# Reading both parts of a bank's maxima in a row, one transpose per quad, and a new table of the order of work

## The chip, the cores and the metric

The kernel runs on one core of a Trainium2 chip. The metric is the device time of one execution in microseconds; a kernel's time is the median over its runs. A core has a matrix engine (TensorE, PE in the profile), three engines for element-wise work (VectorE, or DVE; ScalarE, or ACT; GpSimd, or POOL), an engine that here only issues transfers (SyncE, or SP), and 16 DMA engines. PEld is the loading of weights into TensorE. Matrix products land in PSUM, which has eight banks of 128 partitions x 512 float32 values.

## What is computed

Two attention blocks, A and B, of the same shape work on the same input x (2048 tokens x 640 features); their outputs are mixed by a gate per token. Each block has 32 heads of 20 features and goes through four segments of 512 tokens. Within a segment there is causal softmax attention; across segments a small memory per head is read and updated.

```python
x = A_x
g = _sigmoid((x * gate_w).sum(-1, keepdims=True))
a = _A_ref(x, A_wq, A_wk, A_wv, A_wo, A_beta)
b = _B_ref(x, B_wq, B_wk, B_wv, B_wo, B_beta)
return g * a + (1 - g) * b

# within _A_ref and _B_ref, for each of the N = 4 segments s:
qs, ks, vs = q[:, :, s], k[:, :, s], v[:, :, s]
logits = jnp.einsum("bhqd,bhkd->bhqk", qs, ks) * scale + mask
p = _softmax(logits, axis=-1)
a_dot = jnp.einsum("bhqk,bhkd->bhqd", p, vs)
pq = phi(qs)
num = jnp.einsum("bhld,bhde->bhle", pq, M)
den = jnp.einsum("bhld,bhd->bhl", pq, z)[..., None] + 1e-6
a_mem = num / den
o = g * a_mem + (1.0 - g) * a_dot          # here g = sigmoid(beta), one per head
pk = phi(ks)
M = M + jnp.einsum("bhld,bhle->bhde", pk, vs)
z = z + jnp.einsum("bhld->bhd", pk)
```

## The kernel before

**Windows, quads, slots.** A window is one segment of one block, so there are eight windows. The 32 heads of a window are worked on in eight quads of four heads, so there are 64 quads, numbered 0 to 63. The kernel goes through 66 slots, and in slot i, TensorE does the "T units" of quad i and the "S units" of quad i + 2 (`LEAD` is 2), with "fill" work in between: the projections to q, k and v, the output projections, transposes and the memory's products.

**S units and T units.** Softmax needs each row's maximum before the exponentials. The S units compute the scores of a quad with queries on the partitions, only to find those maxima. A quad has five S units for each half of the array (rows 0 to 63 and 64 to 127 of TensorE's array work side by side, as two lanes); a unit fills one PSUM bank, with one part (512 columns) or two parts (384 and 128, or 256 and 256 columns). VectorE reads each part with one operation that adds the causal mask and takes the maximum (line 1268), which the profile shows as an operation and a short read of the accumulator. The T units compute the scores again, with keys on the partitions and with the maximum subtracted by two extra rows of the contraction; ScalarE takes the exponential of a bank (line 1357), GpSimd clears what lies above the diagonal (line 1358), and the product with the values follows in the next slot (line 1385).

**The way of the maxima.** When all ten banks of a quad's S units are read, `m_unit` splits the maxima into a high part (ScalarE, line 1292) and a low part (GpSimd, line 1293) in a tile `mt` of 128 partitions x 32. `m_ready` then waits for one of two small buffers `mr` of 32 partitions x 128. `turn_rows` has VectorE transpose `mt` into `mr` by four operations of 32 x 32 (line 1304), and `send_rows` has SP issue two transfers that put the rows into the two extra rows of q's tile (line 1316). From then on the quad's T units may run.

**How the order is made.** All instructions are emitted by a planner that runs while the kernel is built. It keeps a clock of its own. `put(engine, cost, emit, then, prio)` queues work on an engine's list (A, D, G, S for ScalarE, VectorE, GpSimd, SP): a free engine takes the entry with the lowest priority number, is counted busy for `cost`, and `then` runs a little later, by 0.26 us on VectorE. `dma` does the same for SP. `at(time, fn)` runs a function at a time of the planner's clock. Each engine on the chip carries out its instructions in the emitted order. So the costs set the order, and the chip's real durations set the time.

**The table.** For each slot `RULES` has the order of its five S and five T units as ten letters, and seven numbers: over what share of the slot they are spread, a load of VectorE above which late work isn't started, two delays for transposes' second halves, spare rows, how much earlier than its mark the slot begins, and how long late work may wait.

**Two reads of a bank.** In `s_unit`, `look` is called when a bank's products are done. With two parts, the read of the second is only put on VectorE's list after the first has ended:

```python
if len(todo) > 1:
    one(*todo[0], lambda: (one(*todo[1], read), read()))
else:
    one(*todo[0], read)
```

**The betas.** Each block's 32 betas are loaded into all partitions near the kernel's start (line 1768, priority 15), and `head_gates` (lines 645 to 651) makes the gates from them with ScalarE and VectorE.

Of the kernel before, what the change touches and what calls it, by code (L numbers as in the profile page):

```python
# [12 lines left out]
F32 = mybir.dt.float32  # L13
# [3 lines left out]
ALU = mybir.AluOpType  # L17
# [20 lines left out]
def r32(ap):  # L38
    return ap.bitcast(F32)
# [3 lines left out]
def tile_gated_mix_infini_attn(  # L43
# [44 lines left out]


    RULES = {  # L90
# [66 lines left out]
    }  # L157
    rule = {}
    DONE = {"A": 0.27, "D": 0.26, "G": 0.22, "S": 0.0}
# [10 lines left out]
    def at(time, fn):  # L170
        heapq.heappush(events, (time, next(seq), fn))
# [40 lines left out]
    def put(e, dur, emit, then=None, prio=5):  # L212
        heapq.heappush(ready[e], (prio, next(seq), dur, emit, then))
        load[e] += first_of(dur)
        start_next(e)

    def dma(us, emit, then=None, prio=5, lat=0.9, some=False, issue=0.44):

        def issued():
            dma_free[0] = max(clk[0] + 0.9, dma_free[0]) + us  # L220
            if not some:
                dma_free[0] = dma_free[1] = max(dma_free[0], clk[0] + 0.9 + us, dma_free[1] + us)
            lands.append(dma_free[0] + LANDED)
            if then:
                at(dma_free[0] + lat, then)

        put("S", issue, emit, issued, prio)
# [69 lines left out]
    def then_all(n, fn):  # L297
        left = [n]

        def one():  # L300
            left[0] -= 1
            if not left[0]:
                fn()

        return one
# [944 lines left out]
    def s_unit(i, n):  # L1250
        t, u, q, k = quad(i)
        if n == 0:
            mx[i] = sb.tile([P, 2, 2, NB], F32, tag="mx", name=f"mx{i}", bufs=3)
            s_left[i] = then_all(2 * len(S_UNITS), lambda: m_unit(i))
        todo = S_UNITS[n]
        for half in range(2):
            sc = bank.free.pop(0)
            r = slice(64 * half, 64 * half + 60)

            def look(half=half, sc=sc):  # L1260
                def end():
                    bank.give(sc)
                    s_left[i]()

                read = then_all(len(todo), end)
                def one(pair, qb, off, then):
                    w = P * (qb + 1)
                    put("D", w / 960.0 + 0.105, lambda: nc.vector.tensor_tensor_reduce(  # L1268
                        out=sc[:, off:off + w], in0=sc[:, off:off + w], in1=tri[:, L - w:],
                        scale=1.0, scalar=LOWEST, op0=ALU.add, op1=ALU.max,  # L1270
                        accum_out=mx[i][:, half, pair, qb:qb + 1],
                    ), lambda: at(clk[0] + 0.05, then), prio=3)

                if len(todo) > 1:
                    one(*todo[0], lambda: (one(*todo[1], read), read()))
                else:
                    one(*todo[0], read)

            for j, (pair, qb, off) in enumerate(todo):
                w = P * (qb + 1)  # L1280
                lane_ops[half].append((mm(w), lambda pair=pair, qb=qb, off=off, w=w, r=r, sc=sc: nc.tensor.matmul(  # L1281
                    sc[:, off:off + w], lhsT=q[r, pair, P * qb:P * (qb + 1)], rhs=k[r, pair, 0:w], start=True, stop=True,
                ), look if j == len(todo) - 1 else None))
# [12 lines left out]

    def m_ready(i):
        m_done.add(i)
        mr_store.want(1, lambda mr: put("D", 0.4, lambda: turn_rows(i, mr), lambda: send_rows(i, mr), prio=1), prio=0)

    def turn_rows(i, mr):
        mt = mts.pop(i).rearrange("p f c n -> p (f c n)")
        for j in range(NB):
            nc.vector.transpose(r32(mr[:, 32 * j:32 * j + 32]), r32(mt[32 * j:32 * j + 32, :]))

    def send_rows(i, mr):
        t, u, q, k = quad(i)

        def sent():
            mr_done.add(i)  # L1310
            mr_store.give(mr)

        done = then_all(2, sent)
        for half in range(2):
            r = 64 * half + 60
            dma(0.3, lambda half=half, r=r: nc.sync.dma_start(
                out=r32(q[r:r + 2, :, :].rearrange("p a (b n) -> p (a b) n", b=NB)),
                in_=r32(mr[16 * half:16 * half + 16, :]),
            ), done, prio=-2, some=True, issue=0.68)
# [445 lines left out]
    bts = [const.tile([P, H], F32, name=f"beta{b}") for b in range(2)]  # L1765
    betas_there = then_all(2, lambda: put("D", 0.6, head_gates, prio=6))
    for b in range(2):
        dma(0.9, lambda b=b: nc.sync.dma_start(out=bts[b], in_=betas[b].partition_broadcast(P)), betas_there, prio=15)
    gate_weights()
    at(75.0, lambda: mix_weights(0))  # L1770
    at(215.0, lambda: mix_weights(1))
# [80 lines left out]
```

## Time and profile before

| what | value |
|---|---|
| runs | 987.46, 987.58, 989.22 us; median 987.58 |
| the profiled execution | 989.17 us, of which span 987.4 us |
| granted TensorE clock | 0.999 of full speed |
| TensorE busy | 977.6 us, 99% |
| VectorE busy | 798.8 us, 81% |
| ScalarE busy | 646.9 us, 66% |
| GpSimd busy | 604.0 us, 61% |
| reads of maxima, line 1268 | 1024 operations, 474.5 us, and 1024 reads of the accumulator, 145.2 us |
| transposes of maxima, line 1304 | 256 operations, 51.0 us |

The span goes from the first to the last instruction on the chip. A row of a group reads: line, engine, operation, written tile <- read tiles, shape, count, then busy time in us, the mean of one in ns, and the idle time of the engine just before, with what ended it. A row of waits reads: engine, tile and line that waited <- who ended the wait: us in total, times, longest. A row of the timeline reads: start in us, duration, engine, line, operation; its last part in brackets is the idle time before it and what ended that. Matmuls are pipelined, so one matmul's duration is longer than the time between two starts.

### The profile page before, as it was taken

Reading aid. Unit: us, or ns where it says so; the run is one execution under the profiler, and the core shown is the slowest. Engines: PE = TensorE matmul, PEld = TensorE weight load, DVE = VectorE, ACT = ScalarE, POOL = GpSimd, SP = SyncE. Lnnn points to the kernel's source line nnn. Section 1 sums busy time; section 2 is a strip of 40 time slices with the busy share of each in tenths; the row PEclk is TensorE's granted clock in tenths of the full one; section 3 lists DMA queues with packets and bytes.
Section 4 is the critical chain, followed back from the end, with each engine's and each line's share of the span. In section 5 each row is a group of like instructions: output and inputs, shape, how many; then the busy total and the mean of one; then the engine's idle time right before and its main releaser. Section 6 shows DMA issues by size and latency. Waiting matters only on the chain.

```text
span 987.4 us, 31435 instructions
## 1 busy us (share of the span) xinstructions
PE 977.6 (99%) x11559; PEld 825.5 (84%) x11559; DVE 798.8 (81%) x2825; ACT 646.9 (66%) x1297; POOL 604.0 (61%) x1042
## 2 busy tenths in 40 slices
PE   9999999999999999999999999999999999999998
PEld 7987888788888888897888988887888887879885
DVE  4697888886798888886889878779778898889964
ACT  5366767766667676766776675765667575686582
POOL 4456646955558664776656575566756576566471
PEclk9999999999999999999999999999999999999999
DMA  7998889998897886976769686698577988778531
GB/s 254 303 291 249 280 246 296 258 287 253 258 299 230 281 240 195 313 234 204 225 207 321 191 260 202 212 304 287 166 216 236 276 274 236 219 227 248 147 98 54
DMA packets 146452, 236.47 MB, mean 239 GB/s; under 512 B 12949, under 2 KB 45882, under 8 KB 145978
## 3 DMA queue, kind: packets, MB, share of 16 engines
q1 hardware_dynamic: 146298, 234.46, 77.2%
q8 instruction: 91, 1.49, 0.6%
q14 instruction: 63, 0.52, 0.2%
HBM read 145.26 MB, written 94.65 MB: 243 GB/s over the span
## 4 chain that ended last, share of the span: by engine, by line
PE 93%; DMA 2%; DVE 2%; POOL 1%; ACT 1%; issue 1%; SPq 0%; POOLq 0%; ACTq 0%
PE bank L818 56%; PE bank L1385 14%; PE bank L1365 8%; PE bank L1281 8%; PE bank L929 3%; PE bank L971 3%; PE bank L1029 1%; DMA kst<-kd 1%; PE bank L868 1%; DMA row<-rowg 1%; DMA row<-dots 1%; PE bank L1210 0%; DMA wst<-in_a_wk_dram 0%; POOL p L1358 0%; DVE bank L1268 0%
## 5 line engine op out<-in xcount | busy, mean ns | idle before, releaser
L1268 DVE CUSTOM_DVE_ANT_0 bank<-bank,tri 128x256 f32<-128x256 f32 (+3 forms) x1024 | 474.5, 520 | 90.3 <-PE bank L1281 81.8
L818 PE MATMUL bank<-row,wh 64*128 64x512 f32 x2308 | 487.4, 401 | 0.9 <-ACT p L1357 0.9
L1357 ACT ACTIVATE p<-bank 128x512 f32<-128x512 f32 x546 | 298.8, 604 | 121.9 <-PE bank L1365 102.2
L818 PEld LDWEIGHTS bank<-row,wh 64*128 64x128 f32 x2308 | 315.5, 185 | 15.5 <-ACT p L1357 1.2
L1358 POOL TENSOR_SCALAR_AFFINE_SELECT p<-p 128x256 f32<-128x256 f32 (+1 forms) x546 | 200.0, 376 | 174.5 <-ACT p L1357 161.0
L818 PE MATMUL bank<-row,wl 64*128 64x512 f32 x1154 | 296.9, 398 | 0.0
L555 POOL TENSOR_TENSOR wl<-wst,wh 128x640 fp32r<-128x640 f32 x115 | 181.0, 1579 | 51.7 <-ACT wh L557 41.6
L818 PEld LDWEIGHTS bank<-row,wl 64*128 64x128 f32 x1154 | 173.4, 185 | 5.8 <-issue 0.2
L818 PE MATMUL bank<-wvh,row 64*128 64x320 f32 (+1 forms) x1280 | 177.8, 312 | 0.1
L1365 PE MATMUL bank<-qst,kst 62*128 62x128 f32 (+3 forms) x1024 | 174.9, 319 | 1.3 <-DVE mx L1268 0.7
L1281 PE MATMUL bank<-kst,qst 60*128 60x384 f32 (+3 forms) x1024 | 173.3, 318 | 1.1 <-DMA kst<-kd 1.1
L818 PEld LDWEIGHTS bank<-wvh,row 64*128 64x128 f32 x1280 | 150.4, 185 | 2.0 <-ACT p L1357 0.4
L1268 DVE DVE_READ_ACCUMULATOR2_ANT mx<- 128x1 f32 x1024 | 145.2, 142 | 0.0
L1385 PE MATMUL bank<-p,vst 128*32 128x256 f32 (+3 forms) x1816 | 139.9, 425 | 0.0
L1365 PEld LDWEIGHTS bank<-qst,kst 62*128 62x128 f32 x1024 | 127.1, 186 | 13.8 <-DVE mx L1268 2.9
L1281 PEld LDWEIGHTS bank<-kst,qst 60*128 60x128 f32 x1024 | 126.4, 185 | 11.5 <-DVE mx L1268 2.2
L1385 PEld LDWEIGHTS bank<-p,vst 128*32 128x32 f32 x1816 | 56.6, 110 | 79.7 <-issue 59.5
L818 PE MATMUL bank<-wvl,row 64*128 64x320 f32 (+1 forms) x640 | 105.7, 311 | 0.0
L557 ACT CAST wh<-wst 128x640 fp32r<-128x640 f32 x119 | 87.3, 745 | 20.2 <-PE bank L818 12.8
L818 PEld LDWEIGHTS bank<-wvl,row 64*128 64x128 f32 x640 | 85.2, 186 | 0.7 <-issue 0.2
L1416 ACT COPY row<-bank 128x512 f32<-128x512 f32 x60 | 35.4, 590 | 65.2 <-PE bank L1385 59.5
L530 POOL TENSOR_TENSOR wvl<-wst,wvh 128x640 fp32r<-128x640 f32 (+1 forms) x48 | 60.2, 1260 | 17.6 <-ACT wvh L674 9.2
(119 smaller groups left out, 1131.5 us busy)
## 6 DMA issues: line engine op xcount, KB each, us to landing
qst<-qd SPq DMA_DIRECT2D x128, 240.0 KB
kst<-kd SPq DMA_DIRECT2D x128, 240.0 KB
qd<-row SPq DMA_DIRECT2D x40, 512.0 KB
kd<-row SPq DMA_DIRECT2D x40, 512.0 KB
dots<-row SPq DMA_DIRECT2D x56, 256.0 KB
wst<-wmix SPq DMA_DIRECT2D x35, 320.0 KB
row<-dots SPq DMA_DIRECT2D x42, 256.0 KB
qd<-row SPq DMA_DIRECT2D x40, 256.0 KB
```

The source lines that it names most:

```text
L530: put("G", 0.77 * n, lambda: nc.gpsimd.tensor_tensor(out=wl[:, a:b, :VN], in0=w3, in1=r32(wh[:, a:b, :VN]), op=ALU.subtract), end, prio=4)
L555: put(lo_eng, lo_cost, lambda: lo.tensor_tensor(out=wl, in0=w3, in1=r32(wh), op=ALU.subtract), end, prio=3)
L557: put("A", 0.625, lambda: nc.scalar.copy(wh, w3), low, prio=6)
L818: return nc.tensor.matmul(bank_of, lhsT=w[ROWS[half]], rhs=x_[ROWS[half]], start=start, stop=stop)
L929: return nc.tensor.matmul(pm[:, a - h0:c - h0, :].rearrange("p h e -> p (h e)"), lhsT=r32(pqTs[t, m][ROWS[half], P * n:P * (n + 1)]), rhs= ...
L1268: put("D", w / 960.0 + 0.105, lambda: nc.vector.tensor_tensor_reduce(out=sc[:, off:off + w], in0=sc[:, off:off + w], in1=tri[:, L - w:], s ...
L1281: lane_ops[half].append((mm(w), lambda pair=pair, qb=qb, off=off, w=w, r=r, sc=sc: nc.tensor.matmul(sc[:, off:off + w], lhsT=q[r, pair, P ...
L1357: put("A", 0.483, lambda: nc.scalar.activation(pt, sc, AF.Exp, scale=SCALE), lambda: (bank.give(sc), put("G", 0.15 + 0.105 * len(todo), la ...
L1358: "G", 0.15 + 0.105 * len(todo), lambda: nc.gpsimd.affine_select(out=blocks, in_=blocks, pattern=[[0, len(todo)], [1, P]], base=0, channel ...
L1365: lane_ops[half].append((mm(w), lambda pair=pair, kb=kb, off=off, w=w, r=r, sc=sc: nc.tensor.matmul(sc[:, off:off + w], lhsT=k[r, pair, P ...
L1385: nc.tensor.matmul(po[32 * j:32 * j + 32, P * kb:], lhsT=vst[t % 2][:, kb, h * E1:h * E1 + 32], rhs=pts[i, n, f][0][:, off:off + w], start ...
L1416: either(0.483, lambda: nc.scalar.copy(r32(oT), po), 0.605, lambda: nc.vector.tensor_copy(r32(oT), po), end, 2)
```

## The change

Four things change.

1. The reads of a bank's parts are emitted together, as one entry of VectorE's list, instead of the second after the first.
2. `turn_rows` is one transpose over 128 partitions into a new tile `turned` (128 x 32, three buffers); then a new function `move_rows` copies its four blocks of 32 x 32 side by side into `mr`, two on ScalarE and two on GpSimd. The buffer `mr` is taken after the turn, and the sends follow both engines' copies.
3. The loads of the betas are queued at 16 us of the planner's clock instead of at its start.
4. All 66 rows of the table are others.

```diff
     RULES = {
-        0: "TTTSSTSTSS 1.01 2.38 0.3 8 0 1.6 1",
-        1: "TSTSTSTSTS 1.01 2.38 0.22 8 1.6 1.6 1",
...
+        0: "TSTSTSTSTS 1.01 2.38 0.3 2 0 2.61 1",
+        1: "TTTSSTSTSS 1.01 2.38 0.3 8 0 1.6 1",
...
-                read = then_all(len(todo), end)
-                def one(pair, qb, off, then):
-                    w = P * (qb + 1)
-                    put("D", w / 960.0 + 0.105, lambda: nc.vector.tensor_tensor_reduce(
-                        out=sc[:, off:off + w], in0=sc[:, off:off + w], in1=tri[:, L - w:],
-                        scale=1.0, scalar=LOWEST, op0=ALU.add, op1=ALU.max,
-                        accum_out=mx[i][:, half, pair, qb:qb + 1],
-                    ), lambda: at(clk[0] + 0.05, then), prio=3)
-
-                if len(todo) > 1:
-                    one(*todo[0], lambda: (one(*todo[1], read), read()))
-                else:
-                    one(*todo[0], read)
+                put("D", sum(P * (qb + 1) for _, qb, _ in todo) / 960.0 + 0.125 * len(todo) - 0.02, lambda: [nc.vector.tensor_tensor_reduce(
+                    out=sc[:, off:off + P * (qb + 1)], in0=sc[:, off:off + P * (qb + 1)], in1=tri[:, L - P * (qb + 1):],
+                    scale=1.0, scalar=LOWEST, op0=ALU.add, op1=ALU.max,
+                    accum_out=mx[i][:, half, pair, qb:qb + 1],
+                ) for pair, qb, off in todo], lambda: at(clk[0] + 0.05, end), prio=3)
...
     def m_ready(i):
         m_done.add(i)
-        mr_store.want(1, lambda mr: put("D", 0.4, lambda: turn_rows(i, mr), lambda: send_rows(i, mr), prio=1), prio=0)
-
-    def turn_rows(i, mr):
+        put("D", 0.24, lambda: turn_rows(i), lambda: mr_store.want(1, lambda mr: move_rows(i, mr), prio=0), prio=1)
+
+    turned = {}
+
+    def move_rows(i, mr):
+        done = then_all(2, lambda: send_rows(i, mr))
+        for e, eng, cost, js in (("A", nc.scalar.copy, 0.24, (0, 1)), ("G", nc.gpsimd.tensor_copy, 0.27, (2, 3))):
+            put(e, cost, lambda eng=eng, js=js: [
+                eng(mr[:, 32 * j:32 * j + 32], turned[i][32 * j:32 * j + 32, :]) for j in js], done, prio=1)
+
+    def turn_rows(i):
         mt = mts.pop(i).rearrange("p f c n -> p (f c n)")
-        for j in range(NB):
-            nc.vector.transpose(r32(mr[:, 32 * j:32 * j + 32]), r32(mt[32 * j:32 * j + 32, :]))
+        turned[i] = sb.tile([P, 32], F32, tag="turned", name=f"turned{i}", bufs=3)
+        nc.vector.transpose(turned[i], r32(mt))
...
     for b in range(2):
-        dma(0.9, lambda b=b: nc.sync.dma_start(out=bts[b], in_=betas[b].partition_broadcast(P)), betas_there, prio=15)
+        at(16.0, lambda b=b: dma(0.9, lambda: nc.sync.dma_start(out=bts[b], in_=betas[b].partition_broadcast(P)), betas_there, prio=15))
```

128 rows, old and new, of the table RULES are left out of this document.

## The prediction

> **What bounds the kernel now.** I read the busy shares of the page first, then the groups of TensorE, the order of TensorE in time, and then the waits, engine by engine.
>
> ```profile
> PE 977.6 (99%) x11559; PEld 825.5 (84%) x11559; DVE 798.8 (81%) x2825; ACT 646.9 (66%) x1297; POOL 604.0 (61%) x1042
> ```
>
> TensorE is busy 99% of the span and VectorE is the next engine with 81%. But a busy TensorE need not be a full one. In the next two fences the groups give the counts, and the timeline gives the pitch, the time from one start to the next in a dense run.
>
> ```profile
> L818 PE MATMUL bank<-row,wh 64*128 64x512 f32 x2308 | 487.4, 401 | 0.9 <-ACT p L1357 0.9
> L818 PE MATMUL bank<-row,wl 64*128 64x512 f32 x1154 | 296.9, 398 | 0.0
> L818 PE MATMUL bank<-wvh,row 64*128 64x320 f32 (+1 forms) x1280 | 177.8, 312 | 0.1
> L1365 PE MATMUL bank<-qst,kst 62*128 62x128 f32 (+3 forms) x1024 | 174.9, 319 | 1.3 <-DVE mx L1268 0.7 <-ACT row L987 0.6
> L1281 PE MATMUL bank<-kst,qst 60*128 60x384 f32 (+3 forms) x1024 | 173.3, 318 | 1.1 <-DMA kst<-kd 1.1
> L1385 PE MATMUL bank<-p,vst 128*32 128x256 f32 (+3 forms) x1816 | 139.9, 425 | 0.0
> L818 PE MATMUL bank<-wvl,row 64*128 64x320 f32 (+1 forms) x640 | 105.7, 311 | 0.0
> ```
>
> ```profile
> 20.91 1.35 PE L818 MATMUL bank<-row,wh 64*128 64x512 f32 x10
> 22.07 1.68 PE L818 MATMUL bank<-wvh,row 64*128 64x322 f32 x20
> 23.56 0.64 PE L818 MATMUL bank<-wvl,row 64*128 64x322 f32 x6
> ```
>
> ```profile
> 61.71 2.29 PE bank L1385 x32
> ```
>
> Ten half-array products of 512 columns take 22.07 - 20.91 = 1.16 us, 0.116 each, where the group's mean of one is 401 ns; twenty of 322 columns take 1.49 us, 0.0745 each. At those pitches (2308 + 1154) x 0.116 = 402 us, (1280 + 640) x 0.0745 = 143 us, the 2048 score products, which are 320 columns wide on average (the mean of the widths in the two tables of units), 2048 x 0.0745 = 153 us, and 64 products with the values at 2.29 us (the row of the chain) = 147 us. That is 844 of 987.4 us. The remaining 143 us hold the smaller kinds of matmul, the head, the tail, and the slack: moments in which only one half of the array streams. The Trainium skill, page "Perfetto Trace Analysis", section "Identifying the Most-Contended Engine", says that matmul busy time is a bad measure of distance to the roofline, since pipelined matmuls overlap; by the pitches above the trace agrees (0.116 us beside 401 ns). So a better order can win more than the busy share lets one think, and a worse one can lose it.
>
> What TensorE is seen to wait for is little, and much of it is ended by VectorE (each row: total us, times, longest):
>
> ```profile
> PE bank L1365 <- DVE mx L1268: 0.7, 2, 0.4
> ```
>
> ```profile
> PEld bank L1365 <- DVE mx L1268: 2.9, 9, 0.8
> ...
> PEld bank L1281 <- DVE mx L1268: 2.2, 10, 0.4
> ...
> PEld bank L1385 <- DVE mx L1268: 1.5, 5, 0.4
> ...
> PEld bank L1365 <- DVE mt L1052: 1.1, 3, 0.5
> ```
>
> These are 0.7 + 2.9 + 2.2 + 1.5 + 1.1 = 8.4 us in which a matmul or its weight load waited for a PSUM bank that VectorE had yet to read.
>
> **Part 1, the turn of a quad's maxima.** Now four transposes at L1304 per quad, one for each 32 partitions:
>
> ```profile
> 501.22 0.84 DVE L1304 STREAM_TRANSPOSE mr<-mt 32x32 f32<-32x32 f32 x4
> 502.09 0.57 DVE L1268 CUSTOM_DVE_ANT_0 bank<-bank,tri 128x384 f32<-128x384 f32 x1
> ...
> 503.09 0.34 DVE L1268 CUSTOM_DVE_ANT_0 bank<-bank,tri 128x128 f32<-128x128 f32 x1
> ...
> 503.34 0.34 DVE L1268 CUSTOM_DVE_ANT_0 bank<-bank,tri 128x128 f32<-128x128 f32 x1
> ```
>
> They don't overlap: four take 0.84 us, 64 quads 53.8 us. One transpose over 128 partitions has the same 32 elements per partition, so I take the same quarter, 0.21 us, 13.4 us in all; its upper bound is 0.84 (if the work grows with the partitions). VectorE loses 40 us of 799, between 0 and 40. The plan that orders the instructions counts 0.4 us for a turn that takes 0.84, so VectorE falls 0.44 us behind its plan 64 times, and the bank reads that come next are late by that; in the new plan 0.24 stands beside 0.21. Added are two copies of 32x32 on ScalarE and two on GpSimd per quad. The nearest rows are the small operations on the same maxima:
>
> ```profile
> L1292 ACT CAST mt<-mx 128x16 fp32r<-128x16 f32 x64 | 13.8, 215 | 38.9 <-DVE mx L1268 31.3 <-DVE mw L943 7.6
> ```
>
> ```profile
> L1293 POOL TENSOR_TENSOR mt<-mx,mt 128x16 fp32r<-128x16 f32 x64 | 14.8, 231 | 47.3 <-ACT mt L1292 47.2
> ```
>
> So 128 x 0.215 = 27.5 us on ScalarE (647 to 674) and 128 x 0.231 = 29.6 us on GpSimd (604 to 634). Both stay under 70% of the span, so as work this hides beside TensorE; as a wait it is the rival below. The row must arrive later by one hand-over, about 0.5 us (two copies of 0.215 and a signal). What covers that is the lead: a quad's maxima are finished in the slot two before the one that uses them, and 64 slots share 987 us, so some 15 us each. If that cover were gone each quad would pay the 0.5 us, 32 us in all. The two sends on the SP queue behind it move by the same:
>
> ```profile
> SPq L1316 <- DVE mr L1304: 70.5, 45, 5.1
> ```
>
> SP's queue already stands still at that place 45 times, 1.6 us each, and the loads of q and k queue behind it; the turn gets 0.63 us shorter and the copies add 0.5, so this wait stays as it is. The small row buffer is taken after the turn instead of before it, so VectorE no longer waits for a free one; I price that at nothing, since the trace names no such wait.
>
> **Part 2, both parts of a bank in a row.** Now a bank with two parts is read, then the other half's bank, then the second parts: in the fence above the 384-wide part of the first bank starts at 502.09 and its 128-wide part only at 503.09, ending about 503.34. In a row the second part would start 0.52 us after the first, as the 384-wide of the other half did; the first bank comes free about 0.5 us earlier and the second no later. Three of five units have two parts, so 192 banks. VectorE's work is unchanged. A lower bound below nothing: another operation can no longer step in between, so a more urgent one waits up to 0.34 us longer; I take no loss from that, since only one part's length is at stake.
>
> Parts 1 and 2 together act on the 8.4 us of waits that VectorE ends. Ends: 0 (TensorE waits next for ScalarE or for the lane's other half) and 8.4. I take half, **4.2 us**: the waits are 0.2 to 0.4 us each on average, of the size of the 0.44 us of lateness and the 0.5 us of earlier release, but they aren't all behind a turn or a two-part bank.
>
> **Part 3, betas later.** Their gates run in the head, on ScalarE, in front of the last casts of x:
>
> ```profile
> 8.14 0.22 ACT L642 ACTIVATE gmem<-beta 128x32 f32<-128x32 f32 x1
> ...
> 10.23 0.20 ACT L642 ACTIVATE gcol<-gcol 128x1 f32<-128x1 f32 x1 [0.35 <-DVE gcol L649]
> 10.34 1.14 ACT L602 CAST row<-row 128x512 fp32r<-128x512 f32 x2
> ```
>
> ```profile
> 10.99 0.19 PEld L868 LDWEIGHTS bank<-row,wh 128*128 128x128 f32 x1 [0.41 <-ACT row L602]
> ```
>
> The gates occupy or block ScalarE from 8.14 to 10.43, and TensorE then waits 0.41 us for the cast behind them. Without them that cast starts when its x has landed. Ends 0 (x lands no earlier) and 0.9 (the other small stalls of the head go too); I take **0.4**. The two issues on SP's queue, the six activations and the small VectorE operations run after 16 us instead, where ScalarE stands idle:
>
> ```profile
> 22.27 1.07 ACT L802 CAST row<-bank 128x512 fp32r<-128x512 f32 x2 [4.75 <-PE bank L818]
> ```
>
> That 4.75 us hides them; on top of busy work they would cost ScalarE about 2.3 us once.
>
> **Part 4, the new table.** It sets per slot the order of score units and when fill work steps in, and it changes nearly everywhere. No row prices it. The stalls of TensorE that VectorE does not end sit at single places of the old order: 0.9, 0.6 and 1.1 us in the groups above, 2.6 us. A new order may lose them or make as many new ones, so the bounds are +2.6 and -2.6 from these rows, and wider from the 143 us of which slack is a part. I take half of the gain, **1.3 us**, because the new order is laid out with durations that stand nearer to the trace's.
>
> Sum: 4.2 + 0.4 + 1.3 = 5.9 us. The profiled execution took 989.17 us, 1.77 over its span and 1.59 above the median of the runs; it would take 983.3, and the median of 987.58 would become **981.7 us**.
>
> **The rivals.**
> *Slower: a late turn now holds ScalarE.* The first copy stands in ScalarE's queue behind a VectorE operation, and behind the copy stand the exponentials that empty banks. An existing wait of that kind:
>
> ```profile
> ACT mt L1292 <- DVE mx L1268: 31.3, 16, 3.3
> ...
> DVE mr L1304 <- POOL mt L1293: 19.5, 24, 2.3
> ```
>
> 16 of 64 waited, 2.0 us each. If 24 of the 64 new copies do so (as many turns wait now for GpSimd, the second row), ScalarE stands 24 x 2.0 = 48 us more. Were a quarter to reach TensorE, 12 us, the time would be 981.7 + 12 = 993.7 us; it decides above 5.9 / 48 = 12% reaching it. For it: queues run in order, as the 31.3 us show. Against it: ScalarE has 340 us of idle time, and the waits that stand in TensorE's groups with ScalarE's name are 0.9 and 0.6 us. The Trainium skill ("TensorE: Matmul & The Clock Gate", section "Architectural detail: the array is 16× 32×32, not 1× 128×128") calls ScalarE and GpSimd strict FIFO, which is this rival's premise; the row of 31.3 us agrees.
> *GpSimd's copies stop VectorE.* If each of the 128 GpSimd copies held VectorE up for its 0.231 us, 29.6 of the 40 us would be given back; a quarter of 4.2 would stay, 1.1 + 0.4 + 1.3 = 2.8, 984.8 us. The rows here don't decide it. The Trainium skill ("Perfetto Trace Analysis", section "Optimizing Scalar/DVE Operations") says that moving work between GpSimd and VectorE might not help, since they share a port; this is that rule's result.
> *No change that can be told.* VectorE isn't the bound at 81%, its waits are replaced by waits for the other half, and the table draws as many new stalls as it removes: 987 us. For it: the visible waits are under 1% of the span.
> *The order wins much.* If the new table with a less loaded VectorE takes a tenth of the 143 us, the time is 973 us. For it: slack of that size exists; against it: what TensorE is seen to wait for is the 8.4 and 2.6 us above, and nothing in the trace says which moments of a half-used array another order would fill.
>
> **How the numbers follow.** The forecast (977 to 985.5 as its own range) gets 0.44, the large gain 0.13, the shared port 0.11, no change 0.15, slower 0.17. Two thousandths of 987.58, 2.0 us, is about what a measurement tells from no change, so faster is under 985.6: 0.44 + 0.13 + 0.11 = 0.68; same 0.15; slower 0.17. The range reaches down to 972, past the large gain's 973, and up to 991, over the half of the slower case that is nearest.
>
> **What would show it.** In the changed kernel's profile: 64 transposes instead of 256, about 0.2 us each; VectorE near 760 us busy; ScalarE near 674 and GpSimd near 634; the pair of reads of a bank back to back; no beta work before 16 us and the head's 0.41 us wait gone; the VectorE rows in TensorE's waits down to about half. Wrong would be: a transpose that takes 0.84 us, a large new row in which ScalarE or GpSimd waits for the turn together with more TensorE waits for ScalarE, or the same VectorE relief with TensorE's slack unchanged.

## The result: 1.2% slower

The changed kernel takes 999.98 us (median of four runs, 998.72 to 1002.11) against 987.88 us; the ratio is 1.0122, with a 95% interval from 1.0101 to 1.0144. The forecast of 981.7 us was wrong in sign, and the time lies above its range.

The busy shares of the changed kernel's page, and the line of its chain of work:

```profile
PE 988.5 (99%) x11559; PEld 823.6 (83%) x11559; DVE 793.8 (80%) x2630; ACT 676.6 (68%) x1429; POOL 630.8 (63%) x1169
...
PE 89%; DVE 5%; DMA 3%; issue 1%; ACT 1%; POOL 0%; SPq 0%; DVEq 0%; ACTq 0%
```

ScalarE and GpSimd carry what the prediction said (674 and 634). VectorE has 195 instructions fewer, as it should, but is only 5 us less busy. In the chain its share is 5% now and was 2% before. The waits of the weight loads say where it comes in (us in total, times, longest):

```profile
PEld bank L1273 <- DVE mx L1265: 8.5, 28, 0.8
PEld bank L1365 <- DVE mx L1265: 6.8, 22, 1.0
...
PEld bank L1385 <- DVE mx L1265: 1.5, 4, 0.4
...
PEld bank L818 <- DVE mx L1265: 1.2, 5, 0.3
```

Before, the first two rows had 2.2 and 2.9 us, and all rows of this kind 7.0 us; now they have 18.4. The waits that were to halve have nearly trebled: TensorE waits longer for banks that VectorE reads. What VectorE does meanwhile, first in the kernel before:

```profile
502.09 0.57 DVE L1268 CUSTOM_DVE_ANT_0 bank<-bank,tri 128x384 f32<-128x384 f32 x1
502.57 0.14 DVE L1268 DVE_READ_ACCUMULATOR2_ANT mx<- 128x1 f32 x1
502.57 0.60 DVE L1268 CUSTOM_DVE_ANT_0 bank<-bank,tri 128x384 f32<-128x384 f32 x1
503.09 0.14 DVE L1268 DVE_READ_ACCUMULATOR2_ANT mx<- 128x1 f32 x1
503.09 0.34 DVE L1268 CUSTOM_DVE_ANT_0 bank<-bank,tri 128x128 f32<-128x128 f32 x1
503.34 0.14 DVE L1268 DVE_READ_ACCUMULATOR2_ANT mx<- 128x1 f32 x1
```

And in the changed kernel:

```profile
506.83 0.57 DVE L1265 CUSTOM_DVE_ANT_0 bank<-bank,tri 128x384 f32<-128x384 f32 x1 [1.60 <-PE bank L701]
507.31 0.14 DVE L1265 DVE_READ_ACCUMULATOR2_ANT mx<- 128x1 f32 x1
507.49 0.30 DVE L1265 CUSTOM_DVE_ANT_0 bank<-bank,tri 128x128 f32<-128x128 f32 x1
507.70 0.14 DVE L1265 DVE_READ_ACCUMULATOR2_ANT mx<- 128x1 f32 x1
507.70 0.60 DVE L1265 CUSTOM_DVE_ANT_0 bank<-bank,tri 128x384 f32<-128x384 f32 x1
508.22 0.14 DVE L1265 DVE_READ_ACCUMULATOR2_ANT mx<- 128x1 f32 x1
508.39 0.30 DVE L1265 CUSTOM_DVE_ANT_0 bank<-bank,tri 128x128 f32<-128x128 f32 x1
508.61 0.14 DVE L1265 DVE_READ_ACCUMULATOR2_ANT mx<- 128x1 f32 x1
```

Compare the starts. When the next read is of another bank and its products are there, it starts together with the read of the accumulator (507.70 and 507.70; before, 503.09 and 503.09). When it is the second part of the same bank, it starts 0.17 to 0.18 us later (508.22 and 508.39). The two parts are different columns, but the read writes its masked scores back into the bank it reads, and in the emitted program the second read of a bank waits on VectorE's own semaphore for the first. In the trace it starts 0.034 us after the accumulator's read has ended. In the kernel before the same wait stands in the program, but the other half's read mostly came between, and it was over by then: of the 354 reads there that have such a wait and come right behind another read, 344 start together with the accumulator's read, and the other ten wait for TensorE. Now 384 start late (64 quads x 3 units x 2 halves), by 0.175 us in the median, 67 us in all.

Most of these 67 us hide in the busy time. The accumulator's read, 0.14 us, ran beside the next read before and now runs alone; that part counts as work. The other 0.034 us of each, 13 us in all, count as idle. So VectorE is taken for 794 + 13 = 807 us, against 799 before. A read that starts late is itself 0.03 us shorter (for 128 columns 0.217 us to its accumulator's read, 0.249 before), so a pair loses 0.14 us and 384 pairs 55 us. The turn gave 40 us and the reads took more: 15 us more by these sums, 8 by the two totals.

### The profile page after: what moved, and what is told of

It reads as the page before. It is cut to its first block, busy times and chain, and to the rows that moved or that the text cites. A ratio compares the mean times of both kernels' runs of the same rounds, so it can differ in the third digit from the quotient of the medians.

```text
span 997.0 us, 31486 instructions
## 1 busy us (share of the span) xinstructions
PE 988.5 (99%) x11559; PEld 823.6 (83%) x11559; DVE 793.8 (80%) x2630; ACT 676.6 (68%) x1429; POOL 630.8 (63%) x1169
## 4 chain that ended last, share of the span: by engine, by line
PE 89%; DVE 5%; DMA 3%; issue 1%; ACT 1%; POOL 0%; SPq 0%; DVEq 0%; ACTq 0%
PE bank L818 52%; PE bank L1385 14%; PE bank L1365 8%; PE bank L1273 7%; PE bank L929 3%; DVE bank L1265 3%; PE bank L971 2%; PE bank L1029 1%; DMA qd<-row 1%; DMA kst<-kd 1%; PE bank L868 1%; DVE mx L1265 1%; DMA kd<-row 1%; DMA wst<-in_a_wk_dram 0%; PE bank L1210 0%
## 5 line engine op out<-in xcount | busy, mean ns | idle before, releaser
L1265 DVE CUSTOM_DVE_ANT_0 bank<-bank,tri 128x384 f32<-128x384 f32 (+3 forms) x1024 | 489.6, 510 | 109.2 <-PE bank L1273 85.2
L818 PE MATMUL bank<-row,wh 64*128 64x512 f32 x2308 | 503.5, 402 | 0.3
L818 PE MATMUL bank<-row,wl 64*128 64x512 f32 x1154 | 307.9, 400 | 0.0
L818 PE MATMUL bank<-wvh,row 64*128 64x320 f32 (+1 forms) x1280 | 190.3, 313 | 0.1
L1365 PE MATMUL bank<-qst,kst 62*128 62x384 f32 (+3 forms) x1024 | 175.4, 323 | 0.7 <-DVE mx L1265 0.6
L818 PEld LDWEIGHTS bank<-wvh,row 64*128 64x128 f32 x1280 | 157.7, 185 | 2.3 <-DVE mx L1265 0.5
L1385 PE MATMUL bank<-p,vst 128*32 128x384 f32 (+3 forms) x1812 | 139.2, 424 | 0.0
L1273 PEld LDWEIGHTS bank<-kst,qst 60*128 60x128 f32 x1024 | 123.7, 185 | 18.4 <-DVE mx L1265 8.5
L818 PE MATMUL bank<-wvl,row 64*128 64x320 f32 (+1 forms) x640 | 110.4, 311 | 0.0
L818 PEld LDWEIGHTS bank<-wvl,row 64*128 64x128 f32 x640 | 89.0, 186 | 0.7 <-issue 0.4
L784 DVE TENSOR_TENSOR row<-bank,row 128x512 fp32r<-128x512 f32 x80 | 54.4, 685 | 16.1 <-ACT row L777 7.9
```

Of the source, the lines that this page charges most:

```text
L784: put("D", 0.605, lambda: nc.vector.tensor_tensor(out=lo, in0=src, in1=r32(hi), op=ALU.subtract), out, prio=1)
L818: return nc.tensor.matmul(bank_of, lhsT=w[ROWS[half]], rhs=x_[ROWS[half]], start=start, stop=stop)
L1265: put("D", sum(P * (qb + 1) for _, qb, _ in todo) / 960.0 + 0.125 * len(todo) - 0.02, lambda: [nc.vector.tensor_tensor_reduce(out=sc[:, of ...
L1365: lane_ops[half].append((mm(w), lambda pair=pair, kb=kb, off=off, w=w, r=r, sc=sc: nc.tensor.matmul(sc[:, off:off + w], lhsT=k[r, pair, P ...
L1385: nc.tensor.matmul(po[32 * j:32 * j + 32, P * kb:], lhsT=vst[t % 2][:, kb, h * E1:h * E1 + 32], rhs=pts[i, n, f][0][:, off:off + w], start ...
```

## The experiments

Times below are medians; to compare runs that were measured at different times I use the ratio to the kernel before, measured beside each, times 988 us. "Same order" means that every engine gets its instructions in exactly the changed kernel's order (or the old one's), so only the named thing differs. Three theories stood at first: W, the wait of VectorE for itself; T, the new table's order is worse; C, ScalarE and GpSimd stand at the copies.

### The wait taken away in the same order (e4_aside)

```diff
-out=sc[:, off:off + w], ...
+out=junk[:, off:off + w] if len(todo) > 1 else sc[:, off:off + w], ...   # junk: bf16, 128 x 512, in SBUF
```

Buffers of `turned`, `mw` and `mt32` went from 3, 4 and 3 to 1, 2 and 2 to make room.

> The changed kernel with every engine's order kept, but the masked scores of a two-part bank are written to a bf16 tile aside instead of back into the bank (the maxima don't change), so that the second read no longer waits for the end of the first. Theory W (the wait of VectorE for itself between the two reads of a bank, 0.175 us x 384 banks, costs the time): the pitch of a pair falls from 0.91 to about 0.77 us, TensorE's waits ended by the maxima fall from 18 to under 8 us, and the time falls from 1000 to 984 to 990 us. Theory T (the new order itself is worse): order unchanged, so 997 to 1002. Theory C (ScalarE and GpSimd stand at the copies): unchanged, 997 to 1002.

Measured: 979.34 us, ratio 0.9902 [0.9879, 0.9925]. That is 1% under the kernel before, 2.2% under the changed kernel, and below the 984 to 990 us of theory W. The timeline of this run:

```profile
499.93 0.56 DVE L1266 CUSTOM_DVE_ANT_0 junk<-bank,tri 128x384 bf16<-128x384 f32 x1 [0.23 <-PE bank L1274]
500.41 0.08 DVE L1266 DVE_READ_ACCUMULATOR2_ANT mx<- 128x1 f32 x1
500.41 0.29 DVE L1266 CUSTOM_DVE_ANT_0 junk<-bank,tri 128x128 bf16<-128x128 f32 x1
500.62 0.08 DVE L1266 DVE_READ_ACCUMULATOR2_ANT mx<- 128x1 f32 x1
500.64 0.56 DVE L1266 CUSTOM_DVE_ANT_0 junk<-bank,tri 128x384 bf16<-128x384 f32 x1
```

The second part now starts with the accumulator's read (500.41), and a pair takes 0.71 us instead of 0.87. Its busy shares, and what the first of the two rows of waits has become:

```profile
PE 969.6 (99%) x11559; PEld 824.1 (84%) x11559; DVE 737.9 (75%) x2630; ACT 674.9 (69%) x1429; POOL 630.9 (65%) x1169
```

```profile
PEld bank L1274 <- DVE mx L1266: 1.0, 2, 0.8
```

T and C fall as the cause of the whole loss: order and copies are unchanged and the loss is gone. That they cost a few us isn't excluded. And two things changed: the wait went, and the write became cheaper (0.48 us for 384 columns instead of 0.51). The next run keeps the cheap write.

### The wait of the pair alone, with the cheap write (e19_pairwait)

```diff
-out=junk[:, off:off + w] if ...
+out=junk[:, (L - w) * half:][:, :w] if ...     # both parts of one bank overlap; of the two halves only the 384-wide parts do
```

> As the run with the scores aside, same order on every engine; both parts of one bank write overlapping columns of the tile aside, and neighbouring banks write different ones, so that, but for about one bank in six, only the second read of a bank waits for the first, as in the changed kernel. Against the run without the wait it gives the price of that wait alone, with the cheap write kept: 384 x 0.12 = 45 us of VectorE at the 0.21 to 0.26 us of time per us of VectorE seen so far, so 989 to 993 us (theory W). If the cheap write made most of the gain: 979 to 984.

Measured: 989.72 us, ratio 1.0012 [0.9999, 1.0025]. The pair in this run, and the row of waits:

```profile
502.49 0.56 DVE L1266 CUSTOM_DVE_ANT_0 junk<-bank,tri 128x384 bf16<-128x384 f32 x1 [1.60 <-PE bank L701]
502.98 0.08 DVE L1266 DVE_READ_ACCUMULATOR2_ANT mx<- 128x1 f32 x1
503.09 0.29 DVE L1266 CUSTOM_DVE_ANT_0 junk<-bank,tri 128x128 bf16<-128x128 f32 x1
```

```profile
PEld bank L1274 <- DVE mx L1266: 4.8, 16, 0.8
```

The wait behind a write to SBUF is shorter, 0.118 us in the median, 384 times, so 45 us. It costs 1.1%, 10.9 us: 0.24 us of time for each us of VectorE. At that price the 55 to 67 us of the changed kernel are 13 to 16 us (an estimate: that its wait costs the same per us), which is more than its whole loss of 12. The rest of the way from 1000 to 979 is the cheaper write and the longer wait, which these runs don't separate.

### More such waits, and in the old order (e10_aside_wait, e13_bwait)

Both parts of every bank write the same columns aside, so nearly each of these reads waits for the one before (new order); and in the kernel before a tile aside in which neighbours overlap (old order).

> As the run with the scores aside, same order on every engine, but both parts write the same columns of the tile aside, so that each read waits for the end of the one before it. It separates the wait from the cheaper write (bf16 to SBUF took 0.483 us for 384 columns where the write into the bank took 0.515). Theory W: the wait alone makes the loss, so 992 to 1003 us. If the cheaper write made the gain: 979 to 984.

> The kernel before, same order on every engine, but the two-part reads write their scores to one tile aside, in which neighbours overlap, so that most of these reads now wait for the end of the read before. Theory W: VectorE gets up to 0.175 us per such read, less 0.03 saved by the write aside, on 768 reads, and the old order slows too: 1000 to 1020 us. If the loss belongs to the new order alone: 985 to 990.

Measured: 1019.81 us, ratio 1.032 [1.0303, 1.0338], and 1007.45 us, ratio 1.0201 [1.0186, 1.0216]. The first is above its range (I had not counted the waits between banks), the second inside. The waits of the first:

```profile
PEld bank L1274 <- DVE mx L1266: 20.5, 50, 0.9
PEld bank L1366 <- DVE mx L1266: 13.8, 40, 0.9
```

The loss comes with the wait in either order, although both runs have the cheap write. In the new order, the time goes up with TensorE's waits for the maxima: all rows of this kind (weight loads) have 3.0 us in e4_aside, 10.7 in e19_pairwait, 18.4 in the changed kernel and 41.1 in e10_aside_wait, and the times are 978, 989, 1000 and 1020 us. The price of VectorE's time isn't fixed, though: reads in e10_aside_wait start late by some 97 us more than in e4_aside, for 41 us of time, 0.4 per us.

### One part of the change by itself (e3_row, e2_split, e1_table), and a null (e14_null)

The kernel before with only the reads in a row; the changed kernel with only the old reads; the kernel before with only the new table; and the kernel before with one number of the table changed:

```diff
-        40: "TSTTSSTSTS 1.073 2.38 0.3 8 0 1.6 1.19",
+        40: "TSTTSSTSTS 1.01 2.38 0.3 8 0 1.6 1.19",
```

> The kernel before with only the reads in a row. Theory W: 384 x 0.14 = 54 us more of VectorE with no relief from the turn, so 1000 to 1010 us. Theories T and C: 985 to 991, as before.

> The changed kernel with the old emission of the two reads (the second queued after the first has ended); new turn, new table, late betas. Theory W: 982 to 991 us, VectorE's wait for itself covered by the other half's read. Theory T: the table is bad, 996 or more. Theory C: 996 or more.

> The kernel before with only the new table. Theory T: 996 to 1002 us. Theories W and C: 985 to 993, some us off the old table only because the order is drawn anew.

> The kernel before with one number of the table changed: slot 40's spread 1.073 to 1.01, which draws the order anew from there on. It measures how much a redrawn order alone moves the time. Theory F (the table fits only the order that it was fitted to): 20 to 60 us slower, as the runs with one part changed were. If these runs were slow by what was changed in them: 985 to 995.

Measured: 1061.62 (1.0734 [1.0696, 1.0771]), 1043.21 (1.0534 [1.0501, 1.0567]), 1091.73 (1.1037 [1.1003, 1.107]) and 1010.64 us (1.0211 [1.0187, 1.0234]). The first three can't be read as parts: all are slower than both kernels, by up to 103 us against the kernel before, and far above every range given for them but the open one of T and C for e2_split. The null shows why: one number in one slot, with nothing else changed, draws the order anew from slot 40 on and costs 21 us. It is one redraw; how far others spread, and that a redraw alone can cost the 53 to 103 us of the three, isn't measured. e2_split had seemed to speak against W; after the null it says little either way. In e1_table, TensorE's own longest waits are single ones, at transposes and at score products, longer than any that either kernel has there:

```profile
PE bank L971 <- DVE row L774: 11.6, 2, 7.7
PE bank L1281 <- DVE mx L1268: 4.7, 3, 3.7
PE bank L971 <- ACT p L1357: 2.5, 4, 1.3
```

They don't add up to 103 us, but TensorE was also slower: the clock granted to it was 0.956 in the mean, against 0.999 before, and low in single stretches (one digit for each fortieth of the span, in tenths, 9 for 0.9 or more):

```profile
PEclk9999996999999999699988999989999999976989
```

If TensorE's work scales with that clock, 4.4% of 1093 us are 48 us (an estimate). TensorE was idle for 40 us of that span, against 10 before, so 30 us more. The rest stays open.

### What the turn is worth (e11_four, e24_oldturn)

Both are the run e4_aside in the same order. In the first the turn is four transposes into `turned` and the copies stay; in the second it is four transposes straight into the row that is sent, without copies:

```diff
-nc.vector.transpose(turned[i], r32(mt))
+for j in range(NB):
+    nc.vector.transpose(turned[i][:, 32 * j:32 * j + 32], r32(mt[32 * j:32 * j + 32, :]))   # turned: 32 x 128
```

> As the run with the scores aside, same order, but the turn is four transposes of 32x32 instead of one of 128x32: 64 x 0.63 = 40 us more of VectorE. If VectorE's time is passed on as in theory W (54 + 26 us of VectorE gave 20.6 us of time, a quarter), 40 us give 10: 989 us. If a turn lies off the path, 979 to 981.

> As the run with the scores aside, same order on every engine, but the old turn: four transposes straight into the row that is sent, no copies on ScalarE and GpSimd. VectorE gets 40 us more, ScalarE 27 and GpSimd 26 us less, and the sends wait for VectorE alone. Theory P (the new turn is a gain by itself): 984 to 990. Theory Q (its copies cost what it saves, as the doubled copies, 10 us, and the four transposes, 8 us, suggest): 977 to 983. Theory R (the copies cost more): under 977.

Measured: 987.69 us, ratio 1.0014 [0.9992, 1.0037], and 991.69 us, ratio 1.002 [0.9997, 1.0043]. The second median lies above the 984 to 990 us of P. By these ratios the old turn costs 11 to 12 us against e4_aside. The busy shares of the second:

```profile
PE 975.8 (99%) x11559; PEld 822.8 (83%) x11559; DVE 782.2 (79%) x2822; ACT 649.4 (66%) x1301; POOL 602.3 (61%) x1041
```

But part of its 12 us is one stop. Eight of its ten runs took 990.8 to 993.4 us at a granted clock of 0.996 or 0.997, and the other two 984.1 and 985.1 us at 1.0 and 0.999. The profile is of one of the eight. In it TensorE stops once for 5.4 us, because a bank's maxima stand behind one operation of VectorE that took 7.82 us, and the granted clock falls to 0.79 and 0.87 in the two stretches of 10 us from 540 us on (the third number from the right):

```profile
537.63 7.82 DVE L1490 TENSOR_TENSOR row<-row,row 128x512 fp32r<-128x512 f32 x1
541.89 3.01 POOL L555 TENSOR_TENSOR wl<-wst,wh 128x640 fp32r<-128x640 f32 x2
546.20 0.50 PE L929 MATMUL bank<-mbd,row 64*128 64x84 f32 x1 [5.39 <-DVE mx L1266]
```

```profile
540.00:550.00 10.00, 4.61 (x35) 3.06 (x36) 9.88 (x16) 4.10 (x8) 5.86 (x7) 0.79 0.51 148
550.00:560.00 10.00, 10.00 (x110) 7.21 (x102) 6.26 (x22) 2.64 (x5) 1.35 (x3) 0.87 0.62 202
```

That the other seven have the same stop, and the two others don't, is inferred from the clock. If so, the old turn without copies costs about 6 us apart from the stop (984.6 us in place of 979.3, each against its own kernel before), and relieving ScalarE and GpSimd is worth 3 to 4 us against the first run. So P holds and the new turn is a gain, of 0.6 to 1.2% in this order. Q and R fall, Q narrowly: the two quicker runs lie 1 to 2 us above its 977 to 983. In the first run 41 us more of VectorE are 9 to 11 us of time (by the medians or by the ratios), 0.2 to 0.3 per us, near the 0.24 of the waits.

### Which engine should copy (e12_copies, e18_gps, e21_sca, e22_gps)

Again e4_aside in the same order: every copy done twice; GpSimd making all four copies of a quad (in 33 of 64 quads ScalarE made all four too, by a slip of mine, so the first GpSimd run is a doubling there); all four on ScalarE alone; all four on GpSimd alone.

> As the run with the scores aside, same order, but each of the four copies of a quad is done twice: ScalarE and GpSimd get about 8 to 14 us more each (by the pitch of 0.12 us, or by 0.2 us). Theory C (the copies on ScalarE and GpSimd cost): 984 to 990. Otherwise 979 to 982.

> As the run with the scores aside, same order, but all four copies of a quad run on GpSimd and none on ScalarE. Doubling all copies cost about 9 us. If ScalarE's share did that: 972 to 977 here. If GpSimd's did: 983 to 990. If neither is special: 978 to 982.

> As the run with the scores aside, same order, but all four copies on ScalarE and none on GpSimd. If GpSimd's copies are what costs (they stand behind weight splits of 1.5 us, and the sends wait for them): 970 to 977. If ScalarE's are: 983 to 992. If it's neither: 978 to 982.

> The mirror image: all four copies on GpSimd, none on ScalarE. If GpSimd's copies cost: 984 to 995, as in the run that doubled them on GpSimd (994). If ScalarE's cost: 970 to 977. If neither: 978 to 982.

Measured: 989.53 us, ratio 1.0016 [1.0003, 1.0028]; 994.01 us, 1.0052 [1.0034, 1.007]; 986.59 us, 0.9982 [0.997, 0.9995]; and 977.3 us, 0.9882 [0.9865, 0.9899]. The shares of the last two, ScalarE alone first:

```profile
PE 975.1 (99%) x11559; PEld 820.0 (83%) x11559; DVE 738.4 (75%) x2630; ACT 699.7 (71%) x1557; POOL 602.7 (61%) x1041
```

```profile
PE 968.4 (99%) x11559; PEld 823.5 (84%) x11559; DVE 740.0 (76%) x2630; ACT 648.9 (67%) x1301; POOL 651.4 (67%) x1297
```

Copies cost where ScalarE makes them: 25 us more on ScalarE, with GpSimd relieved of 28, made it 0.8% slower, and none on ScalarE is as fast as the split, or 2 us faster (the intervals overlap). That GpSimd's copies are the costly ones is refuted. The two runs that double copies were slower by more, 1.1 and 1.5%; in them both engines, or one twice, write the same rows, and I can't say what part of their loss is work and what part is waiting for each other. That rival of the prediction in which GpSimd's copies hold VectorE up is not borne out: VectorE's busy time is 737.9 us with 128 copies on GpSimd and 740.0 with 256. The Trainium skill ("Perfetto Trace Analysis", section "Optimizing Scalar/DVE Operations") warns that moving work between those two may not help; with these small copies it does (977.3 us with GpSimd's copies, 984 to 993 with VectorE's own four transposes), and GpSimd was the better place.

With longer operations of GpSimd it looks otherwise. In the profile of e24_oldturn, the three of eleven operations at L1490 that run beside no TENSOR_TENSOR of GpSimd take 0.68 to 0.69 us. The other eight take 0.68 to 7.82 us, 1.3 in the median. The profile of the first GpSimd run, too, has one such operation of VectorE of 5.03 us, at L1447, with a granted clock of 0.996. That GpSimd's work is what lengthens them is likely but untested.

The last run beats both kernels: 1.2% under the kernel before.

### A lighter VectorE in the old order (e20_bcheap)

The kernel before, same order, the second part of each bank written aside:

```diff
+out=junk[:, 2 * P * half:][:, :w] if then is read and len(todo) > 1 else sc[:, off:off + w], ...
```

> The kernel before, same order, but the second read of a two-part bank writes its scores to the tile aside (bf16, SBUF): 384 x 0.033 = 13 us less of VectorE, no wait added or taken away. At 0.21 to 0.26 us of time per us of VectorE 3 us faster: 984 to 986. It shows whether the old order gains from a lighter VectorE as the new one does; 987 to 989 if not.

Measured: 986.22 us, ratio 0.9982 [0.9973, 0.9992], and VectorE at

```profile
PE 975.6 (99%) x11559; PEld 824.8 (84%) x11559; DVE 779.1 (79%) x2825; ACT 646.4 (66%) x1297; POOL 603.8 (61%) x1042
```

20 us less of VectorE for 1.8 us, where 13 for 3 were expected: the old order gains too, but at 0.09 per us.

## Why the prediction was wrong, step by step

- **Part 2 is the step that failed.** "VectorE's work is unchanged" and "in a row the second part would start 0.52 us after the first": it started 0.66 to 0.69 us after (506.83 to 507.49, 507.70 to 508.39). The 0.52 us were read off two neighbours that work on different banks; nothing in the row stood for a read that comes right behind a write into its own bank. The bound below nothing was drawn from one mishap, an urgent operation that waits 0.34 us once, and not from 0.175 us on every pair. There was also a slip in the count: three of five units on two halves make 384 banks, not 192. In place of waits cut by half, the pairs lost 55 to 67 us of VectorE, and the waits of the weight loads for the maxima rose from 7.0 to 18.4 us. Shown by e4_aside, e19_pairwait and, in the old order, e13_bwait.
- **Part 1, the work right, its worth too low.** One transpose took 0.207 us where 0.21 was taken, and the copies' busy time came within 4 us of the sums. The row of the changed kernel:

```profile
L1304 DVE STREAM_TRANSPOSE turned<-mt x64: 194/207/216, 40.6 to 963.7; 128x32 f32<-128x32 f32 x64
```

  In the new order, with the write aside, this turn is worth 6 to 12 us (e11_four, e24_oldturn), more than the 4.2 us that Parts 1 and 2 were given together. Half of the visible waits was too little for 40 us of VectorE; whether their whole, 8.4 us, was too low a bound these runs leave open.
- **Part 3, 0.4 us, gave about 0.1.** The gates now run at 24 us, off the head. But the last casts of x then wait for x itself:

```profile
9.42 0.62 ACT L602 CAST row<-row 128x512 fp32r<-128x512 f32 x1 [1.03 <-DMA row<-in_xT_dram]
10.36 0.62 ACT L602 CAST row<-row 128x512 fp32r<-128x512 f32 x1 [0.33 <-DMA row<-in_xT_dram]
```

  The last of them starts at 10.36 where the pair stood at 10.34 before. TensorE's last product at L868 in the head starts at 13.55 instead of 13.66 us. The end of the range at which "x lands no earlier" was nearly the answer.
- **Part 4, half of 2.6 us, had the wrong scale.** The null moved 21 us. What the new table gives against the old one with the same code can't be measured by exchanging the two, since each fits its own code; this stays open, as does the betas' share beyond the head.
- **The rivals.** ScalarE does stand at the turn, 17.0 us in 22 waits, where I had put 48 us in 24:

```profile
ACT mr L1299 <- DVE turned L1304: 17.0, 22, 2.6
```

  Taking ScalarE's copies away altogether gave about 2 us (e22_gps against e4_aside), so this is not what made it slower. The rival's time of 993.7 us lies nearer to the result than the forecast does, but the slower outcome came by a mechanism that was not among the rivals.
- **Net.** Without the wait the changed kernel would stand at 1000 less 13 to 16, so 984 to 987 us, at the upper end of the forecast's own range of 977 to 985.5 or just above it. That is an estimate; no run takes the wait away and keeps the write into the bank.

## What to carry to other kernels

Two operations in a row on the same tile, the first of which writes it, are not the sum of two rows of a profile in which other work stood between them: look for the start of the dependent one, and keep an independent operation in between or let the first write elsewhere. Price a busy second engine by what its time is worth (here 0.2 to 0.3 us per us in the new order, 0.09 to 0.4 over all runs), not only by the waits that carry its name. And where an order is drawn by a planner with a fitted table, undo one part only in experiments that keep every engine's order; a null run tells how much a redrawn order costs by itself.

## What the runs showed of the hardware that was not expected

A read of a bank that waits for VectorE's own last operation starts 0.175 us after the accumulator's read when that operation wrote float32 to PSUM, and 0.118 us when it wrote bf16 to SBUF, though nothing else stood between; without such a dependence the two start together. In both cases it starts about 0.034 us after the end of the accumulator's read, and that read takes 0.14 and 0.08 us. The Trainium skill ("VectorE: DVE Perf Modes", section "The TRN2 errata — SBUF-src ops pay a fixed extra latency per instruction") says that SBUF latency is exposed between instructions, so that many small tiles pay it each time. No run here shows that latency by itself; the 0.175 and 0.118 us come on dependent reads alone. And the same masked maximum is cheaper when its scores go to SBUF as bf16: 0.483 us instead of 0.515 for 384 columns, from its start to its accumulator's read.
